# Pooled attention and a maxout FFN on one core: values ahead of late scores, one copy for pooled keys, a last tile split 128 to 384

## The chip, the cores and the metric

The kernel runs on one core of one Trainium2 chip. The metric is the device time of one execution in microseconds (us). Engines are named as in the profile: PE (TensorE; PEld is its weight load), DVE (VectorE), ACT (ScalarE), POOL (GpSimd), SP (SyncE, used here for issuing DMAs).

## The reference

Eight batches of eight heads, 576 tokens, head size 64. Keys and values are pooled over groups of 8 tokens to 72, attention goes from 576 queries to 72 pooled keys, and the result feeds a feed-forward layer in which the hidden value is the largest of three products.

```python
k_p = k.reshape(B, H, Sp, pool, D).mean(axis=3)      # B=H=8, Sp=72, pool=8, D=64
v_p = v.reshape(B, H, Sp, pool, D).mean(axis=3)
scores = np.matmul(q, k_p.transpose(0, 1, 3, 2)) / np.sqrt(D)
attn = softmax(scores)                               # over the 72 pooled keys
x = np.matmul(attn, v_p).transpose(0, 2, 1, 3).reshape(B * S, H * D)   # 4608 x 512
h = np.maximum(np.maximum(x @ w1, x @ w2), x @ w3)   # 512 -> 768
out = h @ w_out                                      # 768 -> 512
```

## The kernel before

**Attention of a batch.** Keys are pooled (kp), transposed (pkt) and laid into a zero-padded array (kz); queries are transposed (pqt to qT). Scores of a head are matmuls into psc, and ACT's exp writes et, which is laid out keys x tokens. A batch has five chunks of 128 tokens; `values(b, c0)` makes one chunk: eight matmuls into pav (64 value columns and the sum of weights), then a reciprocal and a multiplication on DVE give xn. `turn_x` transposes xn in four PE transposes into pxt and copies it to xT (x0 to x4 by ACT; X1 is the same with the copy on DVE). xT holds all tokens as columns. From batch 2 on these turns are DMA transposes on SP.

**Tokens re-ordered.** The rows of q are grouped so that the first 256 columns of et in each head come from the first part of the scores and the other 320 from the second. For batch 0, `scores4(h)` makes the first 256 columns of four heads and `scores2(h)` the other 320 of two heads. Chunks 0 and 1 are columns 0 to 255, so they need only the two scores4.

**Feed-forward.** Blocks of 512 tokens, nine in all. A slot of a block is one product of the hidden layer (w1, w2 or w3 for 128 of 768 hidden columns, four matmuls over the 512 inputs into pw, L299) or one 128-token tile of the output (po, L335). After w1 ACT casts pw to t (L305), after w2 DVE takes the maximum (t1, L308), after w3 DVE takes the maximum into hT (L311). pw, po and several small tiles share three PSUM buffers (tag pw); psc and pav share two (tag att); one more (tag tr) serves the transposes.

Block 0 starts before its 512 columns of xT exist, and is therefore cut into narrow parts:

```python
parts = [(0, 1, 0, 128), (0, 1, 128, 256), (1, 3, 0, 256), (0, 3, 256, NB),
         (3, JCH, 0, NB)]
```

Slots 0 to 2 read columns 0 to 127 of xT, slots 3 to 5 columns 128 to 255, slots 6 to 11 columns 0 to 255, slots 12 to 20 columns 256 to 511, and slots 21 to 29 all 512. Slots 30 to 33 are the four output tiles.

**The order.** It is written out by hand. Each engine runs its instructions in the order in which the program emits them. `block(n, plan)` emits the slots one by one and after each the steps that the plan names for it. A step is a letter and a number: v makes the values of a chunk, x or X turns it, s makes the scores of a head, a adds halves of batch 1's keys on DVE (k16, L281), K pools them on PE (pkp) and copies them to kp, k transposes kp and fills kz, q or Q transposes a part of the queries, T and Z are DMA transposes. Before block 0 come batch 0's scores, pooled values (`pool_v`: sums over 8 tokens by identity matmuls into pvp, and a copy to vp), the first chunk (`first_values`, `first_turn`, each in two halves of four heads) and the second chunk's values. `heat` is a matmul on constant data into a tile that nobody reads.

**Pooled keys of batch 1.** kp holds each pooled key twice (index a). `pool_k` copies pkp to the first half by DVE (L196) and to the second by ACT (L197).

**The last output tile** is made in two pieces of 256 columns. Each is copied by DVE to osb and stored by two DMAs of 64 rows: three of the four are issued by ACT, the other by SP.

Of the kernel before, what the change touches and what calls it, by code (L numbers as in the profile page):

```python
# [14 lines left out]
def kernel(  # L15
# [11 lines left out]
    nc = tc.nc  # L27
# [3 lines left out]
    B, H, S, D = q.shape  # L31
    POOL = 8
    Sp = S // POOL
    C = H * D
# [23 lines left out]
    kts, vts, qbs, kps, qTs, kTs, ets = {}, {}, {}, {}, {}, {}, {}  # L58
# [52 lines left out]
    for i in range(3):  # L111
# [6 lines left out]
        out=wo_sb, in_=moe_w_out.rearrange("(jc p) c -> p jc c", p=128))  # L118
# [33 lines left out]
    def pool_v(b, h, g, tag, evac):  # L152

        pvp = psp.tile([128, g - h, D], F32, name="pvp", tag=tag[0], bufs=tag[1])
        for j in range(POOL):
            nc.tensor.matmul(pvp, identh[0:Sp, :], vts[b][:, h:g, j, :],  # L156
                             start=(j == 0), stop=(j == POOL - 1))
        evac(out=vp_all[:, b, h:g, 0:D], in_=pvp[0:Sp])
# [30 lines left out]
    def pool_k(b, tag):  # L189

        new_kp(b)
        pkp = psp.tile([128, 6, D], F32, name="pkp", tag=tag[0], bufs=tag[1])
        for j in range(4):
            nc.tensor.matmul(pkp, identh[0:96, :], k16[:, :, j, :],  # L194
                             start=(j == 0), stop=(j == 3))
        nc.vector.tensor_copy(out=kps[b][:, :, 0, :], in_=pkp[0:96])  # L196
        nc.scalar.copy(out=kps[b][:, :, 1, :], in_=pkp[0:96])  # L197

    def score(b, h, out, tp, i0, i1):

# [34 lines left out]
    def values(b, c0):  # L235
        pav = psp.tile([128, 2, 512], F32, name="pav", tag="att", bufs=2)
        for h in range(H):
            nc.tensor.matmul(  # L238
                pav[:, h // 4, 65 * (h % 4):65 * (h % 4) + 65],
                ets[b][:, h, c0:c0 + 128], vp_all[:, b, h, :],  # L240
                start=True, stop=True)
        pv = pav[:, :, 0:260].rearrange("p g (h e) -> p g h e", e=65)
        rcp = sb3.tile([128, 2, 4], F32, name="rcp", tag="rcp")
        nc.vector.reciprocal(out=rcp, in_=pv[:, :, :, 64])  # L244
        xn = sb3.tile([128, 2, 4, D], F16, name="xn", tag="xn", bufs=6)
        nc.vector.tensor_tensor(  # L246
            out=xn, in0=pv[:, :, :, 0:D],
            in1=rcp.to_broadcast([128, 2, 4, D]), op=ALU.mult)
        return xn
# [8 lines left out]
    def do(b, steps):  # L258

        for name in steps.split():
            i = int(name[1:] or 0)
            if name[0] in "qQ":
                turn_q(b, *QS[i], nc.vector.tensor_copy if name[0] == "Q"
                       else nc.scalar.copy, TR)
            elif name[0] == "T":
                qTs[b] = sb2.tile([128, 2 * NG, 128], BF16, name="qT", tag="qT")
                nc.sync.dma_start_transpose(  # L270
                    out=qTs[b], in_=qbs[b].rearrange("p hp t d -> p (hp t d)"))
            elif name[0] == "Z":
                kTs[b] = sb2.tile([128, 6, 96], BF16, name="kT", tag="kT")
                nc.sync.dma_start_transpose(
                    out=kTs[b], in_=kps[b].rearrange("p i a d -> p (i a d)"))
            elif name[0] == "k":
                turn_k(b)
            elif name[0] == "K":
                pool_k(b, PW)
            elif name[0] == "a":  # L280
                nc.vector.tensor_tensor(out=k16, in0=kts[b][:, :, 0:4],  # L281
                                        in1=kts[b][:, :, 4:8], op=ALU.add)
            elif name[0] == "s":
                if i == 0:
                    new_et(b)
                scores(b, i)
            elif name[0] == "v":
                xns[b, i] = values(b, CHUNKS[i][0])
            else:
                turn_x(b, *CHUNKS[i], xns[b, i], TR,  # L290
                       nc.vector.tensor_copy if name[0] == "X" else nc.scalar.copy)
# [35 lines left out]
    def project(n, hT):  # L327
        for mm in range(4):
            m = 4 * n + mm
            last = m == TOK // 128 - 1  # L330
            osb = sb3.tile([128, C], F32, name="osb", tag="osb", bufs=5)
            for c in ((slice(0, C // 2), slice(C // 2, C)) if last else (slice(0, C),)):
                po = psp.tile([128, c.stop - c.start], F32, name="po", tag="pw", bufs=3)
                for jc in range(JCH):
                    nc.tensor.matmul(po, hT[:, jc, bass.ts(mm, 128)], wo_sb[:, jc, c],  # L335
                                     start=(jc == 0), stop=(jc == JCH - 1))
                if last:
                    nc.vector.tensor_copy(out=osb[:, c], in_=po)
                else:
                    nc.scalar.copy(out=osb[:, c], in_=po)  # L340
                for u in range(2):
                    b, g = divmod(2 * m + u, NG)
                    dst = out[S * b:S * b + S, :].rearrange("(r g) c -> r g c", g=NG)
                    e = nc.scalar if last and (u or c.start == 0) else nc.sync
                    e.dma_start(out=dst[:, GS[g], c], in_=osb[64 * u:64 * u + 64, c])
            yield
# [7 lines left out]
    def heat(n):  # L354
        for _ in range(n):
            nc.tensor.matmul(wm, warm[:, 0:128], warm, start=True, stop=True)  # L356
# [30 lines left out]
    def scores2(h):  # L387
        psc = psp.tile([128, 2, 512], F32, name="psc2", tag="att", bufs=2)
        for i in range(2):
            score(0, h + i, psc[:, i, 0:64], 0, 4, 5)  # L390
            score(0, h + i, psc[:, i, 64:320], 1, 0, 4)
        exp(ets[0][:, h:h + 2, 256:S], psc[0:Sp, :, 0:320])

    def first_values():

        c0 = 0
        xns[0, 0] = sb3.tile([128, 2, 4, D], F16, name="xn", tag="xn", bufs=6)
        for g in range(2):
            pav = psp.tile([128, 4, 65], F32, name="pav0", tag="pw", bufs=3)
            for h in range(4):  # L400
                nc.tensor.matmul(pav[:, h, :], ets[0][:, 4 * g + h, c0:c0 + 128],
                                 vp_all[:, 0, 4 * g + h, :], start=True, stop=True)
            rcp = sb3.tile([128, 4], F32, name="rcp0", tag="rcp0")
            nc.vector.reciprocal(out=rcp, in_=pav[:, :, 64])
            nc.vector.tensor_tensor(
                out=xns[0, 0][:, g], in0=pav[:, :, 0:D],
                in1=rcp.to_broadcast([128, 4, D]), op=ALU.mult)

    def first_turn(g, tag):
        pxt = psp.tile([128, 2, 128], F16, name="pxt0", tag=tag[0], bufs=tag[1])  # L410
        for kc in range(2):
            nc.tensor.transpose(pxt[:, kc, :],
                                xns[0, 0][:, g, 2 * kc:2 * kc + 2, :], identh)
        nc.scalar.copy(out=xT[:, 2 * g:2 * g + 2, 0:128], in_=pxt)
# [5 lines left out]
    heat(2)  # L420
    scores4(4)
    pool_v(0, 0, 4, PW, nc.vector.tensor_copy)
    scores2(0)
    pool_v(0, 4, 6, PW, nc.vector.tensor_copy)
    pool_v(0, 6, 8, PW, nc.vector.tensor_copy)
    scores2(2)
    first_values()
    scores2(4)
    heat(1)
    first_turn(0, PW)  # L430
    xns[0, 1] = values(0, 128)
    first_turn(1, TR)
    scores2(6)


    def block(n, plan):

        hT = new_hT()
        slot = 0
        for part in (hidden(n, hT), project(n, hT)):  # L440
            for _ in part:
                if slot == 0 and n > 0:
                    pool_work(n, mms[-1])
                for b, steps in plan.get(slot, ()):
                    if b < B:
                        do(b, steps)
                slot += 1

    fold_v(1)
    fold_k(2, nc.gpsimd)  # L450
    block(0, {0: [(0, "X1")], 3: [(0, "v2")], 5: [(0, "v3")], 7: [(0, "x2")],
              9: [(0, "x3")], 12: [(0, "v4")], 15: [(0, "x4"), (1, "a")],
              17: [(1, "K")], 19: [(1, "k")], 21: [(1, "q0")],
              22: [(1, "Q1")], 23: [(1, "Q2 s0")], 24: [(1, "Q3 s1")],
              25: [(1, "s2")], 26: [(1, "s3 s4")], 27: [(1, "s5 s6")],
# [3 lines left out]

    def plan(n):  # L460
        b, i = n + 1, 3 * (n == 1)
        got = {0: [], 3: [], (3 + i if n == 1 else 2): [(b, "k")]}
        got.update({5 + i + h: [(b, f"s{h}")] for h in range(H)})
        got[12 + i].append((b + 1, "T"))
        got.update({14 + i + c: [(b, f"v{c} x{c}")] for c in range(5)})
        got[17 + i].append((b + 1, "Z"))
        if n == 1:
            got[0].append((1, "x3"))
            got[3].append((1, "x4"))
        return got  # L470
# [45 lines left out]
```

## Time and profile before

| what | value |
|---|---|
| median of 5 runs | 241.32 us (240.66 to 245.37) |
| the profiled execution, its own time | 241.03 us |
| its span, first to last instruction | 239.3 us |
| PE busy | 230.0 us, 96% |
| DVE, ACT, POOL busy | 52%, 47%, 52% |
| granted TensorE clock, mean | 0.998 |
| chain that ended last, PE's share | 91% |
| pw (L299) and po (L335) on that chain | 57% and 20% |

The span is cut by the profile in 40 slices of 6.0 us; a digit gives the busy tenths of a slice. In the chain of waits each piece has a start, a duration and what it is; "issue" is a hand-over in which nothing else is seen. In a timeline an instruction has a start, a duration, its engine and line, and what it writes and reads; for merged instructions the duration is that from the first start to the last end. Ends of matmuls are modelled. A slot of four matmuls on 256 columns takes PE 0.44 us from its start to the next one's start; its last result is seen some 0.3 us later.

### The profile page before, as it was taken

What the parts mean: (1) busy time and instruction counts of PE and PEld (TensorE: products, weight loads), DVE (VectorE), ACT (ScalarE), POOL (GpSimd) and SP (SyncE); (2) the same over time, 40 slices, a digit from 0 to 9 for tenths busy, and PEclk for the clock granted to TensorE, in tenths of its full rate; (3) what the DMA queues carried; (4) which work ended last, traced back from release to release, by engine and by line L of the source; (5) the groups of instructions that cost most, each with busy time, mean ns of one, the idle gap of its engine ahead of it and who ended that gap; (6) DMA issues with size and microseconds to landing.
All of it is one profiled execution on the core that took longest, in us unless ns stands there. A gap on an engine that the chain in (4) does not pass through costs nothing.

```text
span 239.3 us, 4200 instructions
## 1 busy us (share of the span) xinstructions
PE 230.0 (96%) x1589; PEld 123.0 (51%) x1591; DVE 123.3 (52%) x231; ACT 111.9 (47%) x184; POOL 123.7 (52%) x91
## 2 busy tenths in 40 slices
PE   7699899999999999999999999999999999999992
PEld 2378755575554555455545554555455544444441
DVE  6767744665672457245724572457245825505521
ACT  2274367546527652765276527652675231142120
POOL 8864266999997569747874688378400000000000
PEclk9999999999999999999999999999999999999999
DMA  7999999999957996699859977997550353034006
GB/s 129 190 196 208 198 201 208 177 167 242 189 113 132 214 188 143 106 223 216 148 97 223 226 157 138 214 198 150 101 132 0 70 125 83 0 76 102 0 21 154
DMA packets 54979, 35.02 MB, mean 146 GB/s; under 512 B 35184, under 2 KB 49520, under 8 KB 54960
## 3 DMA queue, kind: packets, MB, share of 16 engines
q0 software_dynamic: 17088, 17.11, 45.5%
q1 hardware_dynamic: 37632, 17.46, 33.8%
q10 hardware_dynamic: 240, 0.20, 0.4%
q8 instruction: 12, 0.20, 0.3%
q14 instruction: 7, 0.06, 0.1%
HBM read 34.60 MB, written 9.44 MB: 184 GB/s over the span
## 4 chain that ended last, share of the span: by engine, by line
PE 91%; DMA 3%; DVE 2%; ACT 1%; issue 1%; POOL 0%; DVEq 0%; POOLq 0%
PE pw L299 57%; PE po L335 20%; PE psc L203 7%; PE pav L238 4%; DMA qb<-in_q_dram 3%; PE pqt L167 1%; PE pxt L229 1%; PE pvp L156 1%; ACT kz L179 1%; POOL kt L72 0%; DVE k L281 0%; PE pkp L194 0%; DVE t L308 0%; PE pkt L174 0%; PE wm L356 0%
## 5 line engine op out<-in xcount | busy, mean ns | idle before, releaser
L299 PE MATMUL pw<-xT,mw 128*128 128x512 f16 (+2 forms) x708 | 156.1, 361 | 0.2
L299 PEld LDWEIGHTS <-mw 128*128 128x128 f16 x708 | 62.8, 98 | 54.4 <-issue 0.4
L308 DVE TENSOR_TENSOR t<-t,pw 128x512 f16<-128x512 f16 (+2 forms) x59 | 37.8, 641 | 86.6 <-PE pw L299 51.3
L305 ACT CAST t<-pw 128x512 f16<-128x512 f32 (+2 forms) x59 | 32.4, 549 | 44.5 <-PE pw L299 43.1
L335 PE MATMUL po<-mwo,hT 128*128 128x512 f16 (+1 forms) x222 | 49.6, 373 | 0.0
L208 ACT ACTIVATE et<-psc 72x576 f16<-72x576 f32 (+2 forms) x62 | 40.7, 662 | 18.8 <-PE psc L203 18.6
L311 DVE TENSOR_TENSOR hT<-t,pw 128x512 f16<-128x512 f16 (+2 forms) x59 | 37.8, 641 | 9.2 <-PE pw L299 5.2
L340 ACT COPY osb<-po 128x512 f32<-128x512 f32 x35 | 20.5, 585 | 46.0 <-PE po L335 43.9
L135 POOL TENSOR_TENSOR half<-vt 72x2048 f32<-72x2048 f16 x7 | 28.4, 4061 | 12.9 <-DMA vt<-in_v_dram 12.8
L335 PEld LDWEIGHTS <-hT 128*128 128x128 f16 x222 | 20.7, 98 | 22.6 <-DVE hT L311 2.3
L135 POOL TENSOR_TENSOR half<-kt 96x1536 f32<-96x1536 f16 x6 | 18.5, 3086 | 19.0 <-DMA kt<-in_k_dram 19.0
L136 POOL TENSOR_TENSOR half<-half 72x1024 f32<-72x1024 f32 (+1 forms) x13 | 27.2, 2095 | 1.0
L246 DVE TENSOR_TENSOR xn<-pav,rcp 128x512 f16<-128x512 f32 x39 | 27.0, 692 | 1.3
L203 PE MATMUL psc<-qT,kz 128*128 128x64 bf16 (+3 forms) x192 | 25.9, 246 | 0.3 <-DVE kz L179 0.3
L203 PEld LDWEIGHTS <-kz 128*128 128x128 bf16 x192 | 18.0, 98 | 15.6 <-DVE kz L179 0.6
L238 PEld LDWEIGHTS <-et 72*128 72x128 f16 x312 | 15.2, 98 | 7.6
L238 PE MATMUL pav<-vp,et 72*128 72x65 f16 x312 | 16.5, 194 | 0.0
L179 ACT COPY kz<-kT 64x576 bf16<-64x576 bf16 x10 | 11.7, 1168 | 0.9 <-DMA kT<-kp 0.7
L139 POOL TENSOR_TENSOR kp<-half 96x384 bf16<-96x384 f32 x12 | 11.7, 993 | 0.5
L79 POOL DMA_DIRECT2D vt<-in_v_dram x10 | 8.0, 810 | 3.1 <-PE pkp L194 2.1
L244 DVE RECIPROCAL rcp<-pav 128x8 f32<-128x8 f32 x39 | 7.8, 201 | 3.2 <-PE pav L238 3.0
L139 POOL TENSOR_TENSOR vp<-half 72x512 f16<-72x512 f32 x7 | 8.9, 1268 | 0.6
(49 smaller groups left out, 78.7 us busy)
## 6 DMA issues: line engine op xcount, KB each, us to landing
out_dram<-osb SPq DMA_DIRECT2D x70, 128.0 KB, 4.5
kt<-in_k_dram POOLq DMA_DIRECT2D x7, 576.0 KB, 6.6
qb<-in_q_dram POOLq DMA_DIRECT2D x7, 576.0 KB, 11.6
vt<-in_v_dram POOLq DMA_DIRECT2D x7, 576.0 KB, 14.5
mw<-in_moe_w_dram POOLq DMA_DIRECT2D x9, 256.0 KB, 9.4
mwo<-in_moe_w_out_dram POOLq DMA_DIRECT2D x1, 768.0 KB, 18.8
qb<-in_q_dram POOLq DMA_DIRECT2D x2, 288.0 KB, 7.4
xT<-xn SPq DMA_TRANSPOSE x30, 2.4
```

What stands on the lines that cost most here:

```text
L135: e.tensor_tensor(out=f, in0=t[:, :, 0:4, :], in1=t[:, :, 4:8, :], op=ALU.add)
L136: e.tensor_tensor(out=f[:, :, 0:2, :], in0=f[:, :, 0:2, :], in1=f[:, :, 2:4, :], op=ALU.add)
L139: e.tensor_tensor(out=o, in0=f[:, :, 0, :], in1=f[:, :, 1, :], op=ALU.add)
L203: nc.tensor.matmul(out, kz_all[b % 2][:, f % 2, h, :], qTs[b][:, n + i0:n + i1, 64 * (h % 2):64 * (h % 2) + 64], start=True, stop=True)
L208: nc.scalar.activation(out=out, in_=in_, func=FT.Exp, scale=1.0 / 64.0)
L238: nc.tensor.matmul(pav[:, h // 4, 65 * (h % 4):65 * (h % 4) + 65], ets[b][:, h, c0:c0 + 128], vp_all[:, b, h, :], start=True, stop=True)
L246: nc.vector.tensor_tensor(out=xn, in0=pv[:, :, :, 0:D], in1=rcp.to_broadcast([128, 2, 4, D]), op=ALU.mult)
L299: mm = nc.tensor.matmul(pw, w_sb[wi][:, kc, bass.ts(jc, 128)], xT[:, kc, col], start=(kc == 0), stop=(kc == KCH - 1))
L305: nc.scalar.copy(out=t, in_=pw)
L308: nc.vector.tensor_tensor(out=t1, in0=t, in1=pw, op=ALU.max)
L311: nc.vector.tensor_tensor(out=hT[:, jc, c0:c1], in0=t, in1=pw, op=ALU.max)
L335: nc.tensor.matmul(po, hT[:, jc, bass.ts(mm, 128)], wo_sb[:, jc, c], start=(jc == 0), stop=(jc == JCH - 1))
```

## The change

1. Before block 0: the pooled values of heads 4 to 7 are summed right after those of heads 0 to 3 and ahead of scores2(0), and the copy of heads 6 and 7 is ACT's instead of DVE's. The first chunk's values, the second chunk's values and the first chunk's turns come right behind scores2(0). scores2(2) follows the turns; scores2(4) and scores2(6) move into block 0, behind slots 2 and 4 (the new step S).
2. In block 0 the turn of chunk 1 (X1) moves from slot 0 to slot 2, v2 from 3 to 6, v3 from 5 to 7, x2 from 7 to 9, x3 from 9 to 11, and a from 15 to 13. v4 stays at 12, x4 at 15.
3. `pool_k` copies pkp to both halves of kp by one ACT instruction that reads the source twice.
4. The last output tile is made in pieces of 128 and 384 columns.
5. In block 1 step k moves from slot 6 to slot 5.

```diff
-        nc.vector.tensor_copy(out=kps[b][:, :, 0, :], in_=pkp[0:96])
-        nc.scalar.copy(out=kps[b][:, :, 1, :], in_=pkp[0:96])
+        nc.scalar.copy(out=kps[b].rearrange("p i a d -> p a i d"),
+                       in_=pkp[0:96, None].to_broadcast([96, 2, 6, D]))
...
+            elif name[0] == "S":
+                scores2(i)
...
-            for c in ((slice(0, C // 2), slice(C // 2, C)) if last else (slice(0, C),)):
+            for c in ((slice(0, C // 4), slice(C // 4, C)) if last else (slice(0, C),)):
...
     heat(2)
     scores4(4)
     pool_v(0, 0, 4, PW, nc.vector.tensor_copy)
+    pool_v(0, 4, 6, PW, nc.vector.tensor_copy)
+    pool_v(0, 6, 8, PW, nc.scalar.copy)
     scores2(0)
-    pool_v(0, 4, 6, PW, nc.vector.tensor_copy)
-    pool_v(0, 6, 8, PW, nc.vector.tensor_copy)
+    first_values()
+    xns[0, 1] = values(0, 128)
+    first_turn(0, PW)
+    heat(1)
+    first_turn(1, TR)
     scores2(2)
-    first_values()
-    scores2(4)
-    heat(1)
-    first_turn(0, PW)
-    xns[0, 1] = values(0, 128)
-    first_turn(1, TR)
-    scores2(6)
...
-    block(0, {0: [(0, "X1")], 3: [(0, "v2")], 5: [(0, "v3")], 7: [(0, "x2")],
-              9: [(0, "x3")], 12: [(0, "v4")], 15: [(0, "x4"), (1, "a")],
+    block(0, {2: [(0, "S4 X1")], 4: [(0, "S6")], 6: [(0, "v2")], 7: [(0, "v3")],
+              9: [(0, "x2")], 11: [(0, "x3")], 12: [(0, "v4")], 13: [(1, "a")],
+              15: [(0, "x4")],
               17: [(1, "K")], 19: [(1, "k")], 21: [(1, "q0")],
...
-        got = {0: [], 3: [], (3 + i if n == 1 else 2): [(b, "k")]}
+        got = {0: [], 3: [], 2 + i: [(b, "k")]}
```

## The prediction

> **What bounds the kernel now.** I read the page first (shares, slices, chain), then the chain of waits and the timelines of the first 31 us, then busy time by stretch at the end.
>
> ```profile
> PE 230.0 (96%) x1589; PEld 123.0 (51%) x1591; DVE 123.3 (52%) x231; ACT 111.9 (47%) x184; POOL 123.7 (52%) x91
> ...
> PE   7699899999999999999999999999999999999992
> ```
>
> TensorE is busy 96% of the span, and the short slices are the first few and the last. From 31 us on the chain is pw (L299) and po (L335) with hardly a break, so only what delays or frees TensorE before 31 us, or after its last matmul, moves the end. All edits but one lie there (block 1's keys, one slot earlier, lie in full slices). The chain there (start, us, what):
>
> ```profile
> 17.84 0.29 PE pw L299 x2
> 18.13 0.40 PE pxt L229 x4
> 18.53 0.02 issue
> 18.56 0.43 DVE xT L233
> 18.99 0.05 issue
> 19.04 0.40 PE pw L299 x4
> ...
> 26.24 0.88 DVE k L281
> 27.12 0.04 issue
> 27.16 0.82 PE pkp L194 x4
> 27.98 0.02 issue
> 28.01 0.56 DVE kp L196
> 28.57 0.02 issue
> 28.59 0.48 ACT kp L197
> 29.08 0.05 issue
> 29.12 0.44 PE pkt L174 x6
> ```
>
> A chunk of attention reaches the hidden matmuls through four transposes (0.40 to the last result), a copy (0.43 on DVE) and 0.07 of hand-overs: 0.92 us, of which TensorE itself works 0.22. Later, block 0 waits for `a` (the sum k16), and then for two copies of pkp, one after the other. How the slots of block 0 hide such a passage shows on PE's timeline (start, us):
>
> ```profile
> 22.45 0.39 PE L229 MATMUL pxt<-identh,xn 128*128 128x128 f16 x4
> 22.67 1.49 PE L299 MATMUL pw<-xT,mw 128*128 128x256 f16 x12
> 23.99 0.42 PE L238 MATMUL pav<-vp,et 72*128 72x65 f16 x8
> ```
>
> These are x3's transposes, then slots 10, 11, 12, then v4. ACT's copy of x3 runs from 22.91 to 23.50; slot 12, the first to read columns 256 to 511, starts at 23.56. Slots 10 and 11 cover the passage exactly.
>
> The end, by stretches of 1 us (PE, PEld, DVE, ACT, POOL, clock, DMA share, GB/s):
>
> ```profile
> 234.60:235.60 1.00, 0.16 (x2) 0.00 (x0) 0.42 (x1) 0.00 (x0) 0.00 (x0) 1.00 0.98 213
> 235.60:236.60 1.00, 0.00 (x0) 0.00 (x0) 0.00 (x0) 0.00 (x0) 0.00 (x0) 1.00 0.93 217
> 236.60:237.60 1.00, 0.00 (x0) 0.00 (x0) 0.00 (x0) 0.00 (x0) 0.00 (x0) 1.00 0.85 219
> ```
>
> After the last matmul the DMA engines are full with stores.
>
> **Front: scores late, values first.** Unit costs, all from rows of 12 to 31 us. PE spacing: four matmuls of 128 columns 0.22, of 256 columns 0.44; eight of 65 (one v step) 0.26; four of a scores2 0.28; the last result is seen 0.22 to 0.27 later. ACT: exp of 640 columns 0.70, 128x256 copy 0.37, 128x512 copy 0.59, and back to back each starts 0.10 before its predecessor's end. DVE: reciprocal then xn about 0.9; t and hT of 128 columns 0.28, of 256 0.42, 0.10 apart where hT follows t. A hand-over costs 0.03 to ACT or DVE and 0.06 back to PE.
>
> Until slot 0: pool_v of heads 6,7 moves ahead of scores2(0), so its sums end 0.28 earlier, at 15.12; ACT copies them (about 0.27, as its 128x128 cast does) until 15.42; exp of scores2(0), queued behind that copy, has no hurry any more. scores2(0) on PE, then chunk 0's values at 15.24, heads 6 and 7 at 15.47 for that copy. DVE's two reciprocals and xn keep their present spacing and end at 16.75 (now 17.04); transposes 16.81, ACT's copy 17.13 to 17.50. The second half of slot 0 starts at 17.55 instead of 17.84: **0.29 gained**. (Its third weight, issued at 8.94 and 8.7 in landing, is there at 17.6; slot 2 asks at 17.88.)
>
> Slots 0 to 3: exp of scores2(2) sits on ACT ahead of slot 0's t: 17.41 to 18.11, t 18.01 to 18.26. DVE: t1 18.30 to 18.57, hT 18.68 to 18.97. X1 was issued after slot 0 and is now after slot 2, behind those two on DVE: its copy runs 18.88 to 19.30, although its transposes end at 18.78. Slot 3 starts at 19.36 instead of 19.04: 0.32 lost, TensorE standing 0.75. Behind slot 3 on PE stands all else.
>
> Slots 3 to 8: S6 (0.28) is now in here. Slots 3, 4, S6, 5, 6 follow on each other to 20.77. v2 needs exp of S6 (20.29 to 20.99) for heads 6 and 7: 0.08 of wait. Slot 7 at 21.11, v3 21.55, slot 8 at 21.81 (before: 21.57, but with x2 already done). The present wait of slot 7 for t1 of slot 4 (0.24 at 20.9) is gone: DVE does that t1 before v2's xn.
>
> Slots 9 to 12: slot 9 at 22.25, x2 22.69, slot 10 22.91, slot 11 23.35, x3 at 23.80 (when x2's copy has left the one tr buffer). x3 now comes after slot 11 instead of 9, and nothing stands between it and slot 12. Transposes to 24.19, ACT 24.22 to 24.80, slot 12 at **24.86 instead of 23.56**: 1.30 behind, 0.84 of it this naked passage.
>
> Slots 12 to 17: `a` moves from 15 to 13. Its kt landed at 24.6 (issued 13.26, 11.3 to land), so DVE does not stand on a DMA: it runs after t1 of slot 13, 26.94 to 27.89, and pushes hT of slot 14 to 28.23. Slot 17 ends on PE at 27.97; K then has its sum but no free pw buffer until 28.23, and starts at 28.29 (before 27.16): behind by 1.13. The old wait for `a` was 0.50, the new one is 0.32.
>
> Keys: two copies of 384 columns (0.55 + 0.03 + 0.48) become one of 768 on ACT. Rows: 384 columns 0.47, 512 0.59, 640 0.70, 1024 1.02, so 768 lies between 0.70 and 1.02; 0.80 on their line. pkt waits 0.88 after pkp's result instead of 1.15: **0.27 gained**. q0's transposes, after the kz copies, start at 31.77 instead of 30.92.
>
> **Sum: -0.29 + 0.61 + 0.98 - 0.18 - 0.27 = +0.85 us**, where 0.61 is slot 0 to 3, 0.98 slot 3 to 12, 0.18 K's shorter wait (0.50 to 0.32, by rounding 0.17). After q0 the order is the same and PE is full, so it stays. No moved step issues a DMA: batch 0 and 1 are turned by PE and a copy, so SP's and POOL's queues stay as they are, and the last weights (issued 16.6 to 19.3, 16.0 to land) still come a microsecond or more before PE asks. Block 1's keys one slot earlier: zero, covered by slots 5 to 7; without that cover two kz copies on DVE, 1.5 us at most.
>
> **Last tile.** First piece 128 columns instead of 256: its copy ends about 0.45 earlier, ACT issues its two stores earlier, and the third starts at 235.5 instead of 235.9: 0.4 gained if issue decides. The second piece's DVE copy takes 0.55 (row of 384) instead of 0.42, and its stores are 96 KB each instead of 64: at 217 GB/s the further 64 KB are 0.3 us, lost if they come alone. The bytes in all are the same and the DMA engines are 0.85 to 0.98 full: I take 0, ends -0.4 and +0.3.
>
> Against this edit speaks the Trainium skill, "DMA: Bandwidth & Descriptors", section Bandwidth: transfers under 64 KB are dominated by descriptors. The first pieces become 32 KB. Its table has 0.68 us for 4 KB, 0.95 for 64 KB and 6.15 for 1 MB; read between them, a store of 32 and one of 96 KB take 1.93 where two of 64 take 1.90, so by the page the four stores lose under 0.1 (an estimate), and the sum would be +0.9. This trace shows no store below 64 KB; with 64 KB ones among them the stretches kept 217 GB/s beside 213.
>
> Own time of the profiled execution: 241.03 (span 239.3). That makes 241.88; the median of the runs shown is 241.32, 0.29 above, which would make 242.17. I take 242.0, between them.
>
> **Rivals.**
> *Slower, buffers in turn.* If pw buffers are taken in strict turn, slot 11 waits for hT of slot 8 (23.75; +0.46) and slot 17 for slot 14's hT, with K behind it (+0.44): +1.75, 242.9 on the same base. For: DVE is the late engine. Against: slot 17 started at 26.23 though slot 14's hT ended at 26.24.
> *Not slower, the passage is covered.* It decides at slot 12: if x3's copy is done when PE gets there (24.02, so 0.78 earlier than worked out), 0.84 goes and +0.01 is left; with the tail's -0.4 a gain: 240.6 to 241.3. For: ACT is idle there. Against: no work of PE stands between, and slot 12 now starts 0.06 after that copy.
> *The tail is issue-bound* (or byte-bound): -0.4 or +0.3 on the forecast, 241.6 to 242.3.
>
> **Chances.** Forecast with either tail 0.55, buffers in turn 0.22, covered 0.23. A measurement tells about 0.5%, 1.2 us, from no change. The forecast is +0.35%, inside; of it and the other two I give slower 0.30, faster 0.08, within 0.62. Range 240.6 (covered, tail won) to 243.2 (in turn, tail lost).
>
> **What would show it.** PE standing about 0.75 before slot 3 and 0.84 before slot 12; X1's DVE copy after hT; one kp copy of 0.80; K's wait about 0.3; q0 at 31.8. Wrong: slot 12 starting before 24.3, or a PE gap after 32 us that is not in this trace.

## The result, and the profile after

Over 44 executions the changed kernel has a median of 242.47 us (241.74 to 248.62), the kernel before over 79 executions one of 241.68. The medians lie 0.79 us apart. The ratio of the means, without executions over 1.5% above the fastest of their kernel (242.76 beside 241.66), is 1.0046, 95% interval 1.0031 to 1.0061: about 1.1 us slower (0.75 to 1.5), less than 0.5% at its middle, but clear of noise. The forecast was 242.0 and no change that can be told.

The profiled execution of after took 242.21 us, its span is 240.3. Its page, shares and the digits of PE's 40 slices first, then the chain by engine:

```profile
PE 230.7 (96%) x1589; PEld 123.0 (51%) x1591; DVE 122.0 (51%) x229; ACT 112.7 (47%) x185; POOL 123.6 (51%) x91
...
PE   7788999999999999999999999999999999999992
...
PE 39%; DMA 27%; POOL 24%; DVE 3%; issue 2%; ACT 1%; POOLq 0%; DVEq 0%
```

Of the first five digits the second and fifth are one higher and the third and fourth (12 to 24 us) one lower: the edits lie there, but slices of 6 us are too coarse to read their sum from. The chain by engine is a trap. PE had 91% of it and now has 39%, but PE is as busy as before. One wait late in the kernel (at 175 us, shown below) led the backward search off PE into the loads, and from there it could follow POOL and its DMAs for most of the way. A share of the chain says which way the search went, not what the time depends on.

The chain of waits of after between 16 and 32 us (start, us, what):

```profile
17.16 0.73 PE pw L301 x10
...
18.29 0.29 DVE hT L313
18.57 0.35 DVE xT L233
18.92 0.05 issue
18.97 0.62 PE pw L301 x8
...
23.56 0.25 PE pxt L229 x4
23.81 0.02 issue
23.83 0.59 ACT xT L233
24.43 0.04 issue
24.47 0.60 PE pw L301 x4
...
27.41 0.42 DVE hT L313
27.83 0.04 issue
27.88 0.81 PE pkp L194 x4
28.68 0.89 PE pw L301 x8
29.57 0.44 PE pkt L174 x6
```

Waits of PE are counted in this text from start to start: the time between two starts, less what the first instruction takes until the next can start (0.06 for 128 columns, 0.11 for 256). The brackets in the timelines count from the modelled end and are 0.16 to 0.17 shorter.

X1's copy on DVE (18.57) stands behind t and hT, and slot 3 behind it: PE is idle there for 0.76 us. x3's copy (23.83) has nothing beside it, and slot 12 waits 0.84. K waits for hT at 27.41, for 0.30. Then pkt follows pkp with 0.18 of idle PE, where it had 0.44.

PE reached the last scores4 0.41 us earlier in this execution than in that of before (its last matmul starts at 12.68 beside 13.09), because its first loads had landed earlier: the first queries at 8.29 beside 9.36. So the two are compared from the start of that matmul. The end of the last matmul is taken as its start plus 0.11 (256 columns) or 0.16 (384); differences are rounded last:

| time after the last matmul of scores4, us | before | after | difference | worked out |
|---|---|---|---|---|
| second half of slot 0 | 4.76 | 4.48 | -0.28 | -0.29 |
| slot 3 | 5.95 | 6.29 | +0.34 | +0.32 |
| slot 12 | 10.47 | 11.79 | +1.32 | +1.30 |
| K | 14.07 | 15.20 | +1.12 | +1.13 |
| q0 | 17.83 | 18.69 | +0.85 | +0.85 |
| end of the last matmul | 221.51 | 223.20 | +1.69 | +0.85 |
| from there to the end of the span | 4.66 | 4.44 | -0.22 | 0 |

Up to q0 the working holds to 0.02 us. Two rows are off: PE lost another 0.84 us after q0, and the tail gained 0.22. The tail in stretches (columns as in the prediction's tail), and on the timelines of after, then of before:

```profile
235.88:236.88 1.00, 0.16 (x1) 0.00 (x0) 0.56 (x1) 0.00 (x0) 0.00 (x0) 1.00 0.98 217
236.88:237.88 1.00, 0.00 (x0) 0.00 (x0) 0.00 (x0) 0.00 (x0) 0.00 (x0) 1.00 0.88 217
```
```profile
235.43 2.00 ACTq L347 DMA_DIRECT2D out_dram<-osb  x3
236.08 0.56 DVE L340 COPY osb<-po 128x384 f32<-128x384 f32 x1 [0.68 <-PE po L337]
```
```profile
234.60 1.85 ACTq L345 DMA_DIRECT2D out_dram<-osb  x3
234.80 0.42 DVE L338 COPY osb<-po 128x256 f32<-128x256 f32 x1 [0.23 <-PE po L335]
```

ACT issues its three stores from 235.43 on, ahead of PE's end; the last of them starts 0.99 after the last matmul's columns, in before 1.30. The second copy takes 0.56 instead of 0.42. In the two microseconds after the last matmul the DMA engines are as full as before (0.98 and 0.88 beside 0.98 and 0.93), at 217 GB/s beside 213 and 217.

Of the 0.84 us after q0, 0.82 are four waits of PE: 0.10 at 97 us, 0.11 at 117, and 0.13 and 0.48 at 175. The chain at the last one, and ACT's copies there in before:

```profile
170.41 2.40 DMA kT<-kp
...
174.02 1.16 ACT kz L179
175.18 0.03 issue
175.20 0.59 ACT t L307
175.80 0.04 issue
175.84 1.02 PE pw L301 x4
```
```profile
171.19 2.35 ACT L179 COPY kz<-kT 64x576 bf16<-64x576 bf16 x2 [0.42 <-DMA kT<-kp]
```

A transposition of keys lands at 172.81 (before: 171.17). Both kz copies on ACT come late by that, ACT's cast t stands behind them, and w2 or w3 of the next slot wants the buffer that t frees. The experiments have to show whether that belongs to the change.

### The profile page after: what moved, and what is told of

Its sections match the earlier page's. It is cut to its first block, busy times and chain, and to the rows that moved or that the text cites. A ratio compares the mean times of both kernels' runs of the same rounds, so it can differ in the third digit from the quotient of the medians.

```text
span 240.3 us, 4198 instructions
## 1 busy us (share of the span) xinstructions
PE 230.7 (96%) x1589; PEld 123.0 (51%) x1591; DVE 122.0 (51%) x229; ACT 112.7 (47%) x185; POOL 123.6 (51%) x91
## 4 chain that ended last, share of the span: by engine, by line
PE 39%; DMA 27%; POOL 24%; DVE 3%; issue 2%; ACT 1%; POOLq 0%; DVEq 0%
DMA vt<-in_v_dram 25%; PE pw L301 23%; POOL half L135 11%; PE po L337 9%; POOL half L136 7%; POOL vp L139 2%; PE psc L203 2%; DMA kt<-in_k_dram 2%; PE pav L238 1%; POOL qb L86 1%; POOL kt L72 1%; DMA kT<-kp 1%; DVE kf L368 1%; POOL kp L139 1%; PE pqt L167 1%
## 5 line engine op out<-in xcount | busy, mean ns | idle before, releaser
L337 PE MATMUL po<-mwo,hT 128*128 128x512 f16 (+2 forms) x222 | 49.7, 373 | 0.0
L337 PEld LDWEIGHTS <-hT 128*128 128x128 f16 x222 | 20.4, 98 | 22.8 <-DVE hT L313 2.4
L203 PEld LDWEIGHTS <-kz 128*128 128x128 bf16 x192 | 17.9, 98 | 15.7 <-DVE kz L179 0.4
```

Source lines behind the costliest of these rows:

```text
L203: nc.tensor.matmul(out, kz_all[b % 2][:, f % 2, h, :], qTs[b][:, n + i0:n + i1, 64 * (h % 2):64 * (h % 2) + 64], start=True, stop=True)
```

## The experiments

The theory: the front costs what the working says (a copy of X1 behind DVE's queue, a naked passage ahead of slot 12), kp's one copy gives back 0.27, the tail is neutral. The rivals: the slower time comes from the late waits or the tail; or the front's two bad places only stand in for another bound behind them. "Before" or "after" says which kernel is edited. There are twelve runs; all ratios are to before, run on the same chip.

**The keys' copy alone (kp_only), before with the change's `pool_k`.**

> The kernel before with the pooled keys of batch 1 copied by one ACT instruction, nothing else changed. Theory N (TensorE's naked passages in block 0 set the time, and what is gained or lost there reaches the end): one copy of about 0.8 us replaces 0.55 + 0.03 + 0.48, pkt waits 0.25 us less after pkp, time -0.25 us. Rival L (from block 1 on a loop of POOL's fold and the value loads sets the pace, so what happens in block 0 is lost in it): the copy is as short, but the time stays, 0.0 us, with a wait later on that grows by 0.25. Rival E (the kernel is bound by late copies on DVE and ACT): ACT's longer copy delays t of slot 18, 0.0 to +0.2 us.

Ratio 0.9991 (0.9961 to 1.0022). In the profile the wait ahead of pkt is 0.177 instead of 0.445, so 0.27 as worked out, and the ACT copy is 0.795. The time can't tell 0.27 us from nothing. This kernel has late waits too: 1.40 us at 53 us, 0.13 at 97, 0.48 at 175.

**The tail alone (tail_only), before with pieces of 128 and 384.**

> The kernel before with the last output tile in 128 and 384 columns, nothing else changed. The profile of the changed kernel shows 4.41 us from the end of the last matmul's columns to the end of the span against 4.62 before. If that is the edit's and not chance: 4.4 us again and a time 0.2 us shorter (0.1%). If the stores are bound by bytes alone: 4.6 us and no change. If larger stores at the end cost: 4.9 us.

Ratio 0.9989 (0.996 to 1.0018). From the end of the last matmul to the end of the span: 4.43. The five profiles with 256 and 256 columns have 4.62 to 4.72 there, the nine with 128 and 384 have 4.40 to 4.50. So the split gives 0.2 us, in every profile, and does not cost. Late waits here: 0.49 at 126 us and 0.25 at 174.

**X1 back at slot 0 (x1_early), after with**

```diff
-    block(0, {2: [(0, "S4 X1")], 4: [(0, "S6")], ...
+    block(0, {0: [(0, "X1")], 2: [(0, "S4")], 4: [(0, "S6")], ...
```

> The changed kernel with X1, the turn of chunk 1, back behind slot 0 (scores2(4) stays behind slot 2). Theory N: X1's copy runs on DVE ahead of t1 and hT, slot 3 stands no more (0.76 now), slot 7 comes 0.5 to 0.6 us earlier and so does all after it: time -0.55 us against the changed kernel, about +0.5 against before. Rival E: the later waits grow (t1, hT and exps late by the same amount), no more than 0.2 us is gained. Rival L: slot 12 and the first output tile come earlier, but the time does not follow, 0.0 to -0.2.

Ratio 1.0001 (0.997 to 1.0032), where after has 1.0046: moving X1 back takes about 1.1 us off by the times, with 0.3 to 1.9 allowed by the two intervals; 0.55 was expected. The wait of 0.76 ahead of slot 3 is gone, that of 0.84 ahead of slot 12 stays. But two waits stand where the profile of before has none. PE's timeline:

```profile
14.39 0.40 PE L156 MATMUL pvp<-vt,identh 72*128 72x128 f16 x4 [0.20 <-DMA vt<-in_v_dram]
```
```profile
18.39 0.40 PE L301 MATMUL pw<-xT,mw 128*128 128x128 f16 x4 [0.23 <-DMA mw<-in_moe_w_dram]
```

The last value sums wait for the last part of the values (PE idle 0.37 in all there), and slot 2 waits 0.39 for the third weight. They take all that X1's place gave: q0 starts at 31.34 here and at 31.37 in the profile of after, so this profile doesn't show the gain that the times show.

**Both places mended (both_early), x1_early with v3, x2 and x3 one slot earlier, so that slot 11 stands between x3 and slot 12:** `6: v2 v3, 8: x2, 10: x3`.

> As the run before it, and besides v3 behind slot 6, x2 behind 8 and x3 behind 10, so that slot 11 stands between x3's transposes and slot 12. Theory N: the wait ahead of slot 12 falls from 0.84 to about 0.4 us, time -0.95 us against the changed kernel, close to the kernel before (+0.1). Rival E: xn of v3 delays t1 of slot 7 and hT of slot 8, slots 10 and 11 wait for buffers instead, -0.5 in all. Rival L: 0.0 to -0.2.

Ratio 1.0005 (0.9988 to 1.0022): no gain over x1_early is to be seen, though the intervals would hide one of 0.4 us. Its chain:

```profile
22.66 0.57 issue
23.23 0.42 DVE t L310
23.65 0.04 issue
23.69 0.60 PE pw L301 x4
24.29 0.24 PE pxt L229 x4
24.53 0.02 issue
24.55 0.59 ACT xT L233
25.15 0.04 issue
25.19 0.60 PE pw L301 x4
```

The wait ahead of slot 12 falls from 0.84 to 0.40, but slot 10 now waits 0.50 for DVE's t, which stands behind the xn of v2 and v3, made back to back. Here DVE decides, and a wait that was removed came back one place earlier.

**After once more (after_again), no edit.**

> The changed kernel once more, on the chip of the three runs beside it. The first six profiles have the third weight of slot 2 landing at 17.1 to 19.0 us from the start of the span, and only in two of them (17.7 and 17.1, the two that the comparison began with) early enough not to be waited for. Theory W (in a usual execution slot 2 waits for that weight, so the 0.29 us gained before slot 0 is lost, and X1 behind hT of slot 2 adds its whole passage): weight at 18 us or later, slot 2 right after it, slot 3 about 1.1 us after slot 2's start, time +0.9 to +1.2 us against before. Theory N as predicted: +0.65 (0.85 of the front less 0.2 of the tail), whatever the weight does.

Ratio 1.0057 (1.0023 to 1.009); the waits ahead of slots 3 and 12 are 0.75 and 0.84 again. Of waits after q0 this profile has 0.16 us in all against 0.84 in the first profile of the same kernel. The expected wait for the third weight did not come: it landed at 17.9, but this execution was late as a whole (last matmul of scores4 at 14.2), and slot 2 found it there. The time, +1.4 us (0.6 to 2.2), allows both expectations.

**Earlier weights (after_w), after with the first 256 weight columns loaded as two times 128.**

> The changed kernel with the first 256 columns of the three weights loaded as two times 128 columns (three loads more), so that what slots 0 to 5 read lands earlier. From the profiles, a load of 256 KB lands 1.34 us after the one before it, so the third weight's first half should land about 2.0 us earlier, 1.6 if packets of half the size go slower. Theory W: slot 2 no more waits for a weight, slot 0 to 3 come as early as values and evacuations allow, time -0.3 to -0.6 us against the changed kernel beside it. Theory N: no wait for weights was on the path, 0.0 us. A rival of its own: three more issues on POOL (0.77 us each) and smaller packets delay keys and values of batch 1, and it is slower by 0.3 us or more.

Ratio 1.003 (0.9995 to 1.0065), not told apart from after. The waits of 0.76 and 0.84 are there unchanged although the third weight lands at 16.1, so they are not the weight's. The later part of its profile is left out here: that execution took 247.2 us, with PE standing for over 3 us from 126 us on.

**x1_v4: x1_early with v4 put between x3 and slot 12:** `11: [(0, "x3 v4")]`, and 12 empty.

> X1 behind slot 0 as in the run x1_early, and v4 moved from behind slot 12 to behind x3, ahead of slot 12. Its eight matmuls (0.26 us of PE) then lie in the passage of x3, in which PE stands 0.84 us in every profile of this order. Theory N: slot 12 starts as late as now, but with v4 done, the wait shrinks to 0.58, time -0.26 us against x1_early, about -0.2 against before. Rival E: DVE's rcp and xn of v4 (0.9 us) now come ahead of t1 of slot 13 and give a wait at slot 16 or 17 of the same size, 0.0 us.

Ratio 0.9992 (0.9959 to 1.0025), the median 241.15. The eight matmuls of v4 cover 0.26 of the passage, and slot 12 waits 0.58. K's wait is gone. q0 comes 0.08 before that of the kernel before, with 0.33 of wait for the weight in it.

**before_kpt_w: before with the keys' copy, the tail and the split loads.**

> The kernel before with three things: one copy for the pooled keys, the tail of 128 and 384 columns, and the first weights loaded in halves. If the parts add: -0.25 (keys, as measured in the profile of kp_only up to q0) -0.2 (tail) -0.2 (the wait of slots 2 and 3 for the third weight in the profiles of kp_only and tail_only, 0.20 and 0.22) = -0.65 us against before. Rival L (a loop of loads and POOL's folds takes in what the front gains): 0.0 to -0.2.

Ratio 1.0036 (1.0007 to 1.0066): slower, where the other two edits alone were not (0.9991 and 0.9989). The chain shows one place where the split loads cost:

```profile
18.08 15.53 DMA mw<-in_moe_w_dram
33.60 0.05 issue
33.65 1.04 PE pw L299 x4
```

The third weight's first part lands 1.5 us earlier (16.2 instead of 17.7), but the weights of the last columns land about 1 us later (the first at 33.6 instead of 32.6), and PE waits 0.2 for them at 33.6 and again at 36.3. The third weight's middle columns are late too (22.8 instead of 21.9) and cost 0.33 at 22.9. The DMA engines were busy for 80% or more of every slice from 8 to 24 us, so what was put first was most likely taken from what came behind. That the split costs in general is not shown: after_w, the other run with it, was not slower than after, and its last weights landed only 0.4 us later than in after.

**X1 late alone (x1_late), before with** `2: [(0, "X1")]` **instead of** `0: [(0, "X1")]`.

> The kernel before with X1 moved from slot 0 to slot 2, alone. Theory N: X1's copy waits on DVE behind t1 and hT, slot 3 stands about 0.75 us ahead of its start (0.20 to 0.24 now) and starts 0.6 to 0.8 us later; q0 and the end follow: +0.6 to +0.8 us (0.25 to 0.33%). Rival E: later waits shrink in turn (slot 7's 0.24 for t1 of slot 4, K's 0.50), +0.2 us or less.

Ratio 1.0015 (0.9989 to 1.004): the time does not tell it from nothing, nor from what was worked out. The profile does; slot 3 is 0.71 behind:

```profile
8.84 8.90 DMA mw<-in_moe_w_dram
17.75 0.04 issue
17.79 0.41 PE pw L299 x4
18.20 0.02 issue
18.23 0.29 DVE hT L311
18.52 0.37 DVE xT L233
18.89 0.05 issue
18.93 0.40 PE pw L299 x4
```

This is the mechanism by itself: hT, X1's copy, slot 3. And it begins with a weight: slot 2 waits 0.43 for it until 17.75. In kp_only and tail_only, which have X1 behind slot 0, its passage ran beside such a wait (0.20 and 0.22); here it comes after it, and the two add up.

**x3 late alone (x3_late), before with x3 at 11 instead of 9.**

> The kernel before with x3 moved from slot 9 to slot 11, alone. Theory N: PE stands 0.84 us between x3's transposes and slot 12 (0.02 now), q0 comes 0.84 us later, +0.8 us (0.35%) in time. Rival E: the evacuations catch up in that gap and the waits at K (0.50) and pkt (0.45) shrink, +0.3 us.

Ratio 1.0041 (1.0009 to 1.0073), 1.0 us, and in the profile slot 12 and q0 are both 1.00 behind, 0.84 of it the passage and 0.16 a wait between two slots just before it:

```profile
22.95 0.24 PE pxt L229 x4
23.19 0.02 issue
23.21 0.59 ACT xT L233
23.81 0.04 issue
23.85 0.60 PE pw L299 x4
```

It is the same picture as in after at 23.56: one line of the plan carries most of the loss. This kernel, too, has waits of 0.18 and 0.48 at 175 us, with the later blocks of before.

**spread: x1_v4 with S6, v2, v3, x2 and x3 one slot earlier:** `3: S6, 5: v2, 6: v3, 8: x2, 10: x3, 11: v4`.

> The run x1_v4 with scores2(6) behind slot 3 and v2, v3, x2, x3 at 5, 6, 8, 10 (v4 stays behind slot 11): slot 11 and v4, 0.70 us of PE, then stand in x3's passage of 0.84. Theory N: the wait ahead of slot 12 falls from 0.58 to about 0.15, -0.4 us against x1_v4, -0.5 to -0.6 against before (ratio 0.9975). Rival E: DVE has xn of v2 and v3 ahead of t1 and hT of slots 6 to 8, waits of 0.2 to 0.5 appear at slots 6 to 10 as they did at slot 10 in both_early, and nothing is gained.

Ratio 0.999 (0.9962 to 1.0019), the median 241.16. The passage ahead of slot 12 is covered but for 0.14, yet v2 now waits 0.57 at 20.2 for the exp of S6 on ACT. By q0 it is 0.57 behind before, 0.65 behind x1_v4; weight and values landed late in it.

**The front alone (front_only), after with two copies of kp and a tail of 256 and 256.**

> The changed kernel with the two copies of pooled keys and the tail of 256 and 256 columns as before: only the new order of block 0 and before it. If the parts add, as in the prediction's sum: 0.25 us (keys) and 0.2 us (tail) slower than the changed kernel, +1.3 to +1.5 us against before (0.55 to 0.62%), with waits of 0.75 ahead of slot 3 and 0.84 ahead of slot 12 and a wait of 0.45 at pkt. If the order pays elsewhere: less than +1.0.

Ratio 1.0076 (1.0042 to 1.0111), 1.8 us. In its profile q0 is 1.12 behind (worked out: 0.85 + 0.27), with waits of 0.76, 0.84, 0.30 and 0.44, the last again for two copies. After q0 it has no wait that before hasn't.

**The late waits over all kernels.** Idle PE after q0 beyond that of before, in the profiles: none in front_only and both_early; 0.1 to 0.2 us in x1_early, x1_v4 and after_again; 0.5 to 2.2 us in spread, after, tail_only, x1_late, x3_late, kp_only and before_kpt_w (0.46 of its 2.2 for the weights). Four of the last seven differ from before only by an edit in block 0, by the keys' copy or by the tail, and front_only has the whole front and none. So these waits come and go with the execution. Of before there is one profile only, so how often it has them is not known.

## Why the prediction was right, and where it was not

**The case.** What was forecast came: the two new waits are where they were put and 0.76 and 0.84 long (0.75 and 0.84), K waits 0.30 (0.32), the copy of kp takes 0.795 (0.80), and q0 is 0.85 behind. 0.61, 0.98, -0.18 and -0.27 hold in the trace, and the 0.84 in the 0.98 and the -0.27 also by an edit alone. The time, 242.47, lies in the range, and its ratio in the "no change" that the forecast gave. The 0.47 by which 242.0 is short comes from its base: 242.0 less 0.85 is 241.15, from five runs and one profile, and on the 241.68 of 79 executions the same sum gives 242.53. That this is so near is luck in part, for the tail gained 0.22 that the sum had at nothing, and something on the other side, which stays open below, took most of it back. The 0.5% that a measurement was said to need was too much: this one has an interval of 0.15% to each side, and the change is slower.

**The first term, -0.29, and the margin beside it.** The sum put slot 0 0.29 earlier, and let slot 2 find its weight with 0.28 to spare. Both were read from one execution, in which the loads happened to be in time. In four of the twelve profiles of kernels with unsplit weight loads (before, after, after_again, front_only) PE never waits for that weight; their last scores4 start at 12.7 to 14.2 us. In the eight others it starts at 12.3 to 12.65, and slot 2 waits 0.2 to 0.4 us for a weight that lands at 17.7 to 19.0. In five of these eight the value sums wait 0.16 to 0.5 for the last part of the values as well. Where the values are late, slot 0's second half starts no earlier in the new order than in the old (4.95 in x1_early beside 5.02 and 4.94 in kp_only and tail_only), so the 0.29 is gone. Where the weight alone is late (x1_v4), slot 0 does start 0.28 earlier, and slot 2 gives it back in 0.33 of waiting. X1's passage, behind slot 2, is then added to the wait for the weight instead of running beside it (x1_late). That is the term that was mis-sized: for executions in general it should have stood between -0.29 and 0.

**The tail.** 0 was taken, with -0.4 and +0.3 as ends; it is -0.22. Issue decides for the most part: ACT's third store starts 0.31 earlier relative to PE's end, and 0.22 of it arrives. The 64 KB more in the last pieces cost at most the 0.09 between the two. The Trainium skill's "DMA: Bandwidth & Descriptors", section Bandwidth, calls transfers under 64 KB dominated by descriptors, and the estimate from its table (of loads issued by GpSimd) was a loss of under 0.1; the measurement decides, and the tail with pieces of 32 KB came out 0.22 shorter.

**"PE is full, so it stays."** In two profiles it stayed (both_early, front_only), in after it did not: 0.84 was added. A PE gap after 32 us that before's trace doesn't have was named as a sign of being wrong, and it came. The trace of before shows why so little can add it: POOL's loop of issuing the next values (1.35), their landing (14.6) and folding them (7.8) takes 23.75 in all, about as long as a block of PE (24.0), and in before the next issue came only 0.1 to 0.2 us after the fold. The same waits in kernels with an unchanged rest, and their absence in front_only, say that they aren't the change's; they make single profiles differ by up to 2 us.

**What stays open.** Working and tail as measured make 0.85 - 0.22 = +0.63 us. The medians lie 0.79 apart, which leaves 0.16; the means lie 1.1 apart (0.75 to 1.5), which leaves 0.1 to 0.9. Late loads (0.29 and a part of X1's passage) would fit that, but no profile shows them in the change itself: in all three profiles with its front and unsplit loads (after, after_again, front_only) PE does not wait for the weight. x1_early, with X1 out of the way, is at 1.0001, but x1_late came out at +0.4 us (-0.3 to +1.0), which allows the working's value as well as more. Late waits after q0 are in all these times too, and can't be averaged from one profile a kernel. How the rest is shared between these two is not settled.

**The rivals.** Buffers in strict turn: slot 11 and slot 17 have no wait of that kind in after. The covered passage: no; 0.84 stands in every kernel that has x3 at 11 and nothing behind it. Issue-bound tail: true to one half. No kernel here is clearly faster than before; x1_v4, spread and tail_only have the lowest medians, and the intervals of their ratios all hold 1. That the front as a whole costs is shown by front_only, and x3's place by x3_late; what X1's place costs is shown in waits (after, x1_late) and by x1_early's time, not by x1_late's.

## What to carry to other kernels

Where a transfer between engines is hidden by slots of other work, count the slots: a step moved to just ahead of its reader costs its whole passage (0.84 us here), and a copy moved behind two others on its engine costs theirs. Before a gain ahead of a load's first reader is booked, look at how late that load lands in other executions; a margin of 0.3 us read from one profile was there in a third of them. A wait that is taken away at one place comes back at the next where the engine that fed it is itself behind, as DVE in both_early.

## What the runs showed of the hardware

- Loads that queue behind one another land at varying times: the third weight, issued about 8.9 us into the span, at 17.1 to 19.0 us. That spread is larger than any edit here.
- Splitting three loads brought the third weight's first part forward by 1.5 us (17.7 to 16.2) in before_kpt_w and put the last ones back by about 1 us; in after_w it was 1.0 us forward (17.1 to 16.1) and 0.4 us back, each against the profile of the kernel without the split.
- One ACT copy of 768 columns from PSUM took 0.795 us; two of 384 on two engines took 0.55 and 0.48, one after the other.
- The 32 KB stores of the tail were as long on their way as the larger ones: from issue to landing 2.5 us (median of two), beside 2.2 for one of 96 KB. A smaller store did not land sooner after its issue; what was gained is that it was issued sooner.
